# Weight loads of a group issued two periods apart, and the next C chain's x row loaded ahead of the store in SyncE's order

One core of one Trainium2 chip. The metric is the device time of one execution in microseconds (us), the span on the core plus a constant of 1.8 us or so.

## The reference, cut to what matters

```python
def reference(A_x, ..., B_wqkv, B_wo, gate_w):
    x = A_x                                     # 2048 x 1024, bf16
    g = sigmoid((x * gate_w).sum(-1, keepdims=True))
    a = state_space(x, ...)                     # complex scan over 2048 steps, C projection, + x * Dskip
    b = attention(x, B_wqkv, B_wo)              # 32 heads of 32
    return g * a + (1 - g) * b
```

The kernel runs the two branches in one program. Attention is done in 8 groups of 4 heads, with 64 periods to a group; in a period TensorE makes scores, ScalarE (at times with VectorE) exponentiates them, and TensorE fills what is left with the projections and with the state-space branch. The C projection is 32 chains of 16 matmuls. Each chain ends in one 128 x 512 tile in PSUM bank 7.

## The kernel before

A static scheduler in Python emits every instruction with its dependences. Each engine's instructions run in the order of emission, and the waits are put in front of each from the dependences. `p`, the period, is a place in that order.

```python
    def emit(self, eng_name, eng, sems, ...):              # one engine's stream
        for k, o in enumerate(self.q[eng_name]):
            for (l, t) in o.waits:
                eng.wait_ge(sems[l], t * (16 if l.startswith("dma") else 1))
            ins = o.fn(eng)
    # ... cut ...
    def ld_w(self, g, part, eng="sp"):                     # 256 KB of Q, K or V weights, rows of 256 bytes
        ...
        self.S.op(eng, lambda e: e.dma_start(self.w[:, g % 2, part], self.wsrc[:, :, cb:cb + 128]), ...)

    def ld_xn(self, ch, tq, cb):                           # an x row of 128 x 512 in two halves
        for k in range(2):
            self.dma(lambda e, k=k, c0=c0: e.dma_start(self.xn[k], self.x2[...]), [], [("xn", k)] + over, "ld_xn")
        self.c_next += 1

    def skip_ops(self, ch, tq, cb):                        # Ag = x * Dskip * g, two halves, on VectorE
        for k in range(2):
            ops.append((0.335, lambda k=k, c0=c0: self.dve(... self.Ag[:, 0, 256 * k:256 * (k + 1)], self.xn[k] ...
                        [("xn", k), "drow", "g0"], [("Ag", 0)] if k == 0 else [("Ag", 0, 1)], "skip")))
        return ops

    def d_c(self, ch, tq, cb, k):                          # one C chain
        ...
        def evac():
            self.dve(... a = ps[:, 7, :] * g + a ...)      # evac_c: frees bank 7
            self.dma(lambda e: e.dma_start(self.agd[tile], a), [at, ("Ag", 0, 1)], [("agd", tile)], "st_a")
            if self.c_next < 32:
                self.ld_xn(*self.c_list[self.c_next])
    # ... cut: in build(), period p = 64 * g + pg ...
            if pg == (58 if g else 24) and g + 2 < GROUPS:
                for part in (1, 2, 0):
                    self.ld_w(g + 2, part)
```

An evacuation is the VectorE product `evac_c`, which reads bank 7 out; until it has run, TensorE cannot fill the bank again. All of these transfers are issued by SyncE, one after the other; and there is one `Ag` tile, which the skip products write and the stores read.

Of the kernel before, what the change touches and what calls it, by code (L numbers as in the profile page):

```python
# [922 lines left out]
GROUPS = 8  # L923
# [48 lines left out]
class FastPath:  # L972
# [359 lines left out]
    def skip_ops(self, ch, tq, cb):  # L1332

        tt = 4 * ch + tq
        ops = []
        for k in range(2):
            c0 = 512 * cb + 256 * k
            ops.append((0.335, lambda k=k, c0=c0: self.dve(lambda e: e.scalar_tensor_tensor(self.Ag[:, 0, 256 * k:256 * (k + 1)], self.xn[k], self.gcol[:, 0, tt:tt + 1],
                                                                                            self.drow[:, c0:c0 + 256], ALU.mult, ALU.mult),
                                                           [("xn", k), "drow", "g0"], [("Ag", 0)] if k == 0 else [("Ag", 0, 1)], "skip")))  # L1340
        return ops

    def fold_ops(self, j):
# [160 lines left out]
    def d_c(self, ch, tq, cb, k):  # L1504
        ps, xT, cT = self.ps, self.xT, self.cT
        b = self.hp_of[ch]
        hp = self.hp_in[b]
        tt = 4 * ch + tq
        mms = []
        for j in range(8):  # L1510
            for ri in range(2):
                mms.append((1, lambda e, f, l, j=j, ri=ri: e.matmul(ps[:, 7, :], hp(tq, ri, j), cT[ri][:, j, 512 * cb:512 * (cb + 1)], start=f, stop=l),  # L1512
                            [("hp", b, j, ri, tq if b else 0), ("cTf", ri, j)]))


        a = self.Ag[:, 0, :]
        at = ("Ag", 0)
        tile = 2 * tt + cb

        def evac():  # L1520
            self.dve(lambda e: e.scalar_tensor_tensor(a, ps[:, 7, :], self.gcol[:, 0, tt:tt + 1], a, ALU.mult, ALU.add), [("bank", 7), "g0", ("Ag", 0, 1)], [at], "evac_c")  # L1521
            self.dma(lambda e: e.dma_start(self.agd[tile], a), [at, ("Ag", 0, 1)], [("agd", tile)], "st_a")
            if self.c_next < 32:
                self.ld_xn(*self.c_list[self.c_next])
            self.c_left[ch] -= 1
            self.c_end = self.p
        return self.chain(mms, "c", evac)
# [266 lines left out]
    def build(self):  # L1794
# [19 lines left out]
        for j in range(8):  # L1814
            self.bg2 += self.table_ops(j)
        proj = {g: [self.d_qk(g, 1, c) for c in range(4)] + [self.d_v(g, f) for f in range(4)] + [self.d_qk(g, 0, c) for c in range(4)]
                for g in range(1, GROUPS)}
# [27 lines left out]
        outs, k = [], 0  # L1845
# [4 lines left out]
        cur = None  # L1850
# [9 lines left out]
        for p in range(first, NBURST):  # L1860
            g, pg = divmod(p, 64)
# [36 lines left out]
                self.ld_d()  # L1898
                self.ld_xn(*self.c_list[0])

            if pg == (58 if g else 24) and g + 2 < GROUPS:
                assert g or not (proj[0] or cur and cur.tag == "proj")
                for part in (1, 2, 0):
                    self.ld_w(g + 2, part)
            wsv = self.d["B_wo"].rearrange("(a p) n -> p a n", p=128)
            if p == 437:
                self.dma(lambda e: e.dma_start(self.wo3[0], wsv[:, 0:3, :]), [], ["wo0"] + [("w", 0, q) for q in range(3)] + self.x_toks(0), "ld_wo")
# [18 lines left out]
            while used < quota:  # L1926
                if cur is None:
# [16 lines left out]
                    elif kind == "c":  # L1944
                        ok = self.items_done >= 8 * (cs[0][0] + 1) and p > self.item_p + 1 and len(self.folded) == 8

                        def take():
                            self.bgx, self.bgx_at = cs[0][1].pre(), p + 2
                            return cs.pop(0)[1]
# [6 lines left out]
                    cur = take()  # L1956
# [5 lines left out]
                if not cur.pieces:  # L1962
                    ended = cur
                    cur = None
# [247 lines left out]
```

## Time and profile before

| | before |
|---|---|
| time | 924.16 us (median of 3: 923.58 to 925.99) |
| span of the profiled run | 922.4 us |
| busy: ScalarE, TensorE, VectorE | 98%, 98%, 82% |
| ScalarE's waits after the opening and before the end | 3.3 us in five places, 1.0 and 1.6 of them at 246 and 581 us |
| VectorE idle for x rows at the skip products | 12.3 us in 12 places |

In the rows of waits that follow, "A <- B: t, n, m" says that A stood idle t us in all, n times, at most m us, and that B released it. A row of the timeline has start, duration, engine, line, operation, tiles, and in brackets the idle time before it and its releaser. Line numbers above 1340 differ by one to three between the kernels because lines were added and taken out. The granted clock is the share of TensorE's full clock that the trace records as given.

### The profile page before, as it was taken

How to read it: one execution, taken by the hardware profiler on the slowest of the kernel's cores; microseconds unless marked ns; L12 is line 12 of the kernel's file. 1: busy time of each engine (PE TensorE's matmuls, PEld its weight loads, DVE VectorE, ACT ScalarE, POOL GpSimd, SP SyncE). 2: the span in 40 equal slices, each digit the busy share in tenths (PEclk: the TensorE clock that was granted, in tenths of full speed). 3: DMA queues.
4: the chain of work that ended last, by engine and by line, in shares of the span. 5: the costliest groups of instructions: out<-in, count | busy, mean ns of one | idle time of the engine just before them, and what ended most of it. 6: DMA issues, size and time to landing. Idle time of an engine off the chain costs nothing.

```text
span 922.4 us, 33601 instructions
## 1 busy us (share of the span) xinstructions
PE 903.8 (98%) x15188; PEld 515.8 (56%) x15188; DVE 758.1 (82%) x1369; ACT 904.5 (98%) x1034; POOL 6.5 (1%) x31
## 2 busy tenths in 40 slices
PE   8999999999999999999999999999999999999996
PEld 4556655755475555565557555456655655555553
DVE  2799999999989889999889975669989866676665
ACT  6999999999999999999999999999999999999997
POOL 0000000000000000000000000000000000000000
PEclk9999999999999999999999999999999999999999
DMA  9546822223302334122132113123330122533322
GB/s 205 106 83 106 134 50 31 46 45 72 80 9 56 59 62 93 41 41 53 50 82 43 42 40 93 36 69 53 50 65 8 52 76 69 166 87 123 118 65 75
DMA packets 166436, 65.35 MB, mean 71 GB/s; under 512 B 146704, under 2 KB 154896, under 8 KB 166288
## 3 DMA queue, kind: packets, MB, share of 16 engines
q1 hardware_dynamic: 164128, 62.62, 30.8%
q8 instruction: 120, 1.97, 0.9%
q10 hardware_dynamic: 2160, 0.53, 0.3%
q14 instruction: 28, 0.23, 0.1%
HBM read 21.24 MB, written 12.58 MB: 37 GB/s over the span
## 4 chain that ended last, share of the span: by engine, by line
PE 71%; ACT 22%; DVE 4%; SPq 1%; DMA 1%; issue 1%; DVEq 0%
PE f_ps L1766 20%; ACT f_pt L1694 18%; PE f_ps L1678 14%; PE f_ps L1484 12%; PE f_ps L1452 11%; PE f_ps L1512 8%; PE f_ps L1472 6%; ACT f_ub L1717 1%; SPq L1080 1%; DMA f_xa<-in_A_x_dram 1%; DMA f_xT<-in_A_x_dram 1%; ACT f_Et L1694 1%; ACT f_cT_re L1694 1%; DVE f_Ag L1521 1%; ACT f_cT_im L1694 0%
## 5 line engine op out<-in xcount | busy, mean ns | idle before, releaser
L1694 ACT ACTIVATE f_pt<-f_ps 128x1024 bf16<-128x1024 f32 x848 | 801.4, 1138 | 2.7 <-PE f_ps L1678 2.6
L1766 PEld LDWEIGHTS f_ps<-f_V,f_pt 128*128 128x128 bf16 x6784 | 235.0, 96 | 136.6 <-issue 86.6
L1766 PE MATMUL f_ps<-f_V,f_pt 128*128 128x33 bf16 x6784 | 288.4, 178 | 0.2
L1678 PE MATMUL f_ps<-f_Q,f_K 32*128 32x256 bf16 x4096 | 217.7, 273 | 3.9 <-ACT f_cT_re L1694 1.2
L1678 PEld LDWEIGHTS f_ps<-f_Q,f_K 32*128 32x128 bf16 x4096 | 70.2, 92 | 122.8 <-ACT f_pt L1694 62.0
L1484 PE MATMUL f_ps<-f_xT,f_wb 128*128 128x512 bf16 x512 | 131.0, 377 | 1.6 <-DVE f_Ag L1521 0.9
L1452 PE MATMUL f_ps<-f_xT,f_wb 128*128 128x512 bf16 x464 | 119.0, 378 | 3.1 <-DVE f_Ag L1521 3.0
L1398 DVE TENSOR_TENSOR_SCAN f_ht<-f_pf,f_init,f_ut 128x512 bf16<-128x512 f32 x64 | 80.9, 1274 | 0.0
L1512 PE MATMUL f_ps<-f_cT_re,f_hp 128*128 128x512 bf16 x192 | 72.6, 378 | 0.3 <-DVE f_Ag L1521 0.3
L1512 PE MATMUL f_ps<-f_cT_im,f_hp 128*128 128x512 bf16 x192 | 72.5, 378 | 0.0
L1718 DVE TENSOR_SCALAR f_wb<-f_ps 128x512 f32<-128x512 f32 x77 | 52.8, 686 | 23.6 <-PE f_ps L1678 23.0
L1541 PE MATMUL f_ps<-f_wb,f_OT 128*128 128x512 bf16 x252 | 65.5, 378 | 0.0
L1472 PE MATMUL f_ps<-f_wb,f_xT 128*128 128x128 bf16 x896 | 59.1, 219 | 0.0
L1484 PEld LDWEIGHTS f_ps<-f_xT,f_wb 128*128 128x128 bf16 x512 | 40.2, 96 | 33.4 <-issue 1.2
L1717 ACT ACTIVATE f_wb<-f_ps 128x512 bf16<-128x512 f32 x77 | 53.4, 693 | 1.1 <-PE f_ps L1678 1.0
L1452 PEld LDWEIGHTS f_ps<-f_xT,f_wb 128*128 128x128 bf16 x464 | 36.2, 96 | 31.5 <-issue 3.1
L1725 DVE SCALAR_TENSOR_TENSOR f_wb<-f_Ag,f_wb 128x512 int16<-128x512 f32 x77 | 52.6, 684 | 0.7
L1724 DVE SCALAR_TENSOR_TENSOR f_Ag<-f_wb,f_Ag 128x512 f32<-128x512 uint16 x77 | 52.7, 684 | 0.6
L1723 DVE SCALAR_TENSOR_TENSOR f_Ag<-f_wb 128x512 f32<-128x512 uint16 x77 | 52.6, 683 | 0.1
L1472 PEld LDWEIGHTS f_ps<-f_wb,f_xT 128*128 128x128 bf16 x896 | 50.4, 97 | 0.1
L1547 DVE SCALAR_TENSOR_TENSOR f_xT<-f_ps,f_gcol,f_hp 128x512 bf16<-128x512 f32 (+1 forms) x28 | 21.0, 750 | 26.6 <-PE f_ps L1541 26.6
L1390 DVE TENSOR_TENSOR f_tq<-f_ht,f_Et 128x1024 bf16<-128x1024 bf16 x64 | 42.5, 684 | 0.3
(143 smaller groups left out, 876.8 us busy)
## 6 DMA issues: line engine op xcount, KB each, us to landing
ag_scratch<-f_Ag SPq DMA_DIRECT2D x32, 256.0 KB, 2.0
f_hp<-ag_scratch SPq DMA_DIRECT2D x32, 256.0 KB, 2.8
f_wb<-in_B_wqkv_dram SPq DMA_DIRECT2D x21, 256.0 KB, 4.1
out_dram<-f_xT SPq DMA_DIRECT2D x16, 256.0 KB, 2.1
f_xa<-in_A_x_dram SPq DMA_DIRECT2D x32, 64.0 KB, 2.4
f_pf<-in_A_x_dram SPq DMA_DIRECT2D x32, 64.0 KB, 3.2
f_wb<-in_B_wo_dram SPq DMA_DIRECT2D x1, 1024.0 KB
f_OT<-f_On SPq DMA_TRANSPOSE x63, 2.3
```

Of the source, the lines that this page charges most:

```text
L1398: ops.append((1.192, lambda ri=ri: dve(lambda e: e.tensor_tensor_scan(ht[:, ri, :], rr, ut[:, ri, :], self.init[:, ri, j:j + 1], ALU.mult, ...
L1452: mms.append((1, lambda e, f, l, a=a: e.matmul(ps[:, bank, :], w[:, g % 2, part, a, :], xT[:, a, 512 * ch:512 * (ch + 1)], start=f, stop=l ...
L1472: m = e.matmul(ps[:, bank, 128 * q:128 * (q + 1)], xT[:, a, 128 * kt:128 * (kt + 1)], w[:, g % 2, 2, a, :], start=(a == 0), stop=(a == 7))
L1484: mms.append((1, lambda e, f, l, a=a: e.matmul(ps[:, 7, :], bT[:, n % 2, ri, a, :], xT[:, a, 512 * ch:512 * (ch + 1)], start=f, stop=l), [ ...
L1512: mms.append((1, lambda e, f, l, j=j, ri=ri: e.matmul(ps[:, 7, :], hp(tq, ri, j), cT[ri][:, j, 512 * cb:512 * (cb + 1)], start=f, stop=l), ...
L1541: mms.append((1, lambda e, f, l, j=j: e.matmul(ps[:, 7, :], OT[:, j, 256 * qb + 128 * r:256 * qb + 128 * (r + 1)], wo[j][0][:, 512 * cb:51 ...
L1678: m = e.matmul(ps[:, 2 * sl[z] + h % 2, 256 * kl:256 * (kl + 1)], K[32 * h:32 * h + 32, g % 2, 128 * kt:128 * (kt + 1)], Q[32 * h:32 * h + ...
L1694: self.act(lambda e: e.activation(self.tile[p], ps[:, 2 * s:2 * s + 2, :], ACT.Exp, bias=OCTAVES * LN2, scale=LN2 / 128), [("S", s)], [("p ...
L1717: self.S.op("act", lambda e: e.activation(t[:, 0, :], ps[:, 2 * s, :], ACT.Exp, bias=OCTAVES * LN2, scale=LN2 / 128), reads=[("S", s)], wr ...
L1718: self.S.op("dve", lambda e: e.tensor_scalar(xi, ps[:, 2 * s + 1, :], BITS_0, BITS_MIN, ALU.add, ALU.max), reads=[("S", s)], writes=[("xi" ...
L1724: (0.603, lambda: self.dve(lambda e: e.scalar_tensor_tensor(xw, lo, CUBE_C, xw, ALU.add, ALU.mult), [I, W], [W], "exp_c")),
L1766: m = e.matmul(ps[:, 6, o:o + 33], self.tile[p][:, h2, 256 * kl + 128 * qt:256 * kl + 128 * (qt + 1)], V[:, g % 2, 2 * i + kl, h, :], star ...
```

## The change

The intent is that the x row is not late any more: the weights are not to stand in one block in front of it, and it goes out as soon as the buffer that it fills is free.

```diff
@@ skip_ops
+        ops.append((0.0, lambda: self.c_next < 32 and self.ld_xn(*self.c_list[self.c_next])))
         return ops
@@ d_c, evac
             self.dma(lambda e: e.dma_start(self.agd[tile], a), [at, ("Ag", 0, 1)], [("agd", tile)], "st_a")
-            if self.c_next < 32:
-                self.ld_xn(*self.c_list[self.c_next])
             self.c_left[ch] -= 1
@@ build
-            if pg == (58 if g else 24) and g + 2 < GROUPS:
-                assert g or not (proj[0] or cur and cur.tag == "proj")
-                for part in (1, 2, 0):
-                    self.ld_w(g + 2, part)
+            if g + 2 < GROUPS:
+                assert g or pg != 24 or not (proj[0] or cur and cur.tag == "proj")
+                for k, part in enumerate((1, 2, 0)):
+                    if pg == (58 + 2 * k if g else 24):
+                        self.ld_w(g + 2, part)
```

## The prediction

> **What bounds the kernel now.** I read the page first: section 1 and the two large groups of section 5.
>
> ```profile
> PE 903.8 (98%) x15188; PEld 515.8 (56%) x15188; DVE 758.1 (82%) x1369; ACT 904.5 (98%) x1034; POOL 6.5 (1%) x31
> ...
> L1694 ACT ACTIVATE f_pt<-f_ps 128x1024 bf16<-128x1024 f32 x848 | 801.4, 1138 | 2.7 <-PE f_ps L1678 2.6
> ```
>
> ScalarE's exponentials are the pace. One lasts 1138 ns in the record, but in the timeline 15 in a row span 13.99 us, so one starts every 0.91 to 0.93 us and they overlap. I took the starts of all ScalarE instructions from the trace and added up what exceeds 0.933 us after a full exponential and 0.493 us after a half one: most stretches of 30 us lose 0.2 to 0.4 us, but 240 to 270 loses 1.61 and 570 to 600 loses 2.22. So ScalarE bounds the kernel nearly everywhere, and an ScalarE wait in mid-kernel goes straight into the end time. The waits of ScalarE over the whole span are few:
>
> ```profile
> ACT f_pt L1694 <- PE f_ps L1678: 2.6, 4, 1.6
> ACT f_wb L1717 <- PE f_ps L1678: 1.0, 1, 1.0
> ```
>
> The five other rows of that view are the opening (4.5 and 2.7), the last evacuations (1.4 and 0.2) and one of 0.2 near 45 us, which no edited line touches. Asking for the waits in windows of 15 us places the rest: 1.0 at 246, 1.6 at 581, 0.2 at 295, 0.3 at 351, and 0.6 near 10 in the opening. TensorE waits just before each, all for the evacuation of a C chain (L1521): 1.3, 1.6, 0.4 and 0.5 us. Next question: why was that evacuation late? VectorE and the SyncE queue around the largest one:
>
> ```profile
> 569.71 2.06 SPq L1088 DMA_DIRECT2D f_wb<-in_B_wqkv_dram  x3
> 571.81 2.34 SPq L1522 DMA_DIRECT2D ag_scratch<-f_Ag  x1
> 574.19 0.43 SPq L1329 DMA_DIRECT2D f_xa<-in_A_x_dram  x1
> 574.67 0.45 SPq L1329 DMA_DIRECT2D f_pf<-in_A_x_dram  x1
> ...
> 577.08 0.48 DVE L1338 SCALAR_TENSOR_TENSOR f_Ag<-f_xa,f_gcol,f_drow 128x256 f32<-128x256 bf16 x1 [1.81 <-DMA f_xa<-in_A_x_dram]
> 577.49 0.68 DVE L1723 SCALAR_TENSOR_TENSOR f_Ag<-f_wb 128x512 f32<-128x512 uint16 x1
> 578.09 0.47 DVE L1338 SCALAR_TENSOR_TENSOR f_Ag<-f_pf,f_gcol,f_drow 128x256 f32<-128x256 bf16 x1
> 578.49 0.68 DVE L1724 SCALAR_TENSOR_TENSOR f_Ag<-f_wb,f_Ag 128x512 f32<-128x512 uint16 x1
> 579.09 0.74 DVE L1521 SCALAR_TENSOR_TENSOR f_Ag<-f_ps,f_gcol,f_Ag 128x512 f32<-128x512 f32 x1
> ```
>
> The reader sees one queue: three weight loads, the store of the finished C tile, then the two halves of the x row. The store's issue takes 2.34 us where the usual one takes 0.33, so the x row goes out at 574.19; the skip product that needs it idles VectorE for 1.81 us, and the C evacuation stands behind it on the same engine. The chain's last matmul started at 576.82, the evacuation at 579.09: 2.27 us later, where an undisturbed one follows after 0.41. The same happens once more at 234 to 244 (weight loads 234.42 to 236.24, store issue 1.05 us, x row at 237.38, landing after about 3.5 us, skip idle 1.06, evacuation 1.83 us after its last matmul). Of the 32 C chains only these two have a wait for an x row that shows on TensorE. The waits at 295 and 351 have an evacuation 1.1 us late with no wait for a transfer: there the skip products and an exponential's polynomial are simply in front of it.
>
> **What the Trainium skill says.** "Perfetto Trace Analysis", DMA Instruction — HWDGE: the recorded window of such an issue is descriptor generation and its lock, and engines start consuming early when more descriptors are generated than fit the buffer. I read the 2.34 us store issue as that buffer being full of weight descriptors; the trace agrees in that the two stores right behind weights took 1.05 and 2.34 us to issue against a median of 0.33; it does not show the buffer itself. "DMA: Bandwidth & Descriptors", Why small descriptors are slow, charges a fixed cost for each packet; the weight load moves rows of 256 bytes, and its 256 KB land in 4.1 us (median) against 2.0 for a 256 KB C tile with long rows. The same page, Queues, rings and completion order: descriptors of a ring are consumed in order, so an x row behind 768 KB of weights is late; 3.5 and 2.9 us at the two places against a median of 2.4. "PSUM — Partial Sum Buffer", Engine vs sequencer instructions: VectorE's queue is strict FIFO, and the 1.81 us above do hold back an evacuation that does not need the x row.
>
> **The change part by part.** No instruction is added or removed on TensorE, ScalarE or VectorE, and their order is the same: the new entry in the skip list has cost 0 and only issues loads. 62 of the 64 x half-row loads move (the first pair does not), and 10 of the 18 weight loads inside the loop: the second and third of five groups. The group at 51.8 us keeps one period.
> 1. Weight loads at periods 58, 60 and 62 of a group. A period is about 1.85 us (two exponentials), so the second and third go 3.7 and 7.4 us later. Ahead of the store stands one load: 0.58 us of issue in place of 1.8 to 2.06, and a third of the descriptors. The weights are not needed before the next group's first K chain, which starts at about 244.4, against 238.5 for a K part issued at 234.42 with 4.1 us of landing; this part does not move. The Q part, now at about 242, is first read near 279. No new wait there.
> 2. The x row goes out after the second skip product rather than behind the next store. At the first place that product ends near 234.98, so the halves go at about 235.0 and 235.5 (before 237.38, 237.86) and land, with 2.4 to 3.3 us, by 238.8 at the latest; the skip would have started at 240.89 - 1.06 = 239.83. At the second it ends at 570.45, the halves go at 570.5 and 571.0, landing by 574.3; wanted at 577.08 - 1.81 = 575.27. A reserve of 1 us at both.
>
> What that gives. First place: the skip, two products and a sum all move up by 1.06, evacuation at 243.49 - 1.06 = 242.43, that is 0.77 after the last matmul. Chain 1 had 0.69 and cost TensorE nothing, chain 19 had 1.00 and cost 0.31 on TensorE and 0.06 on ScalarE. So 1.01 of ScalarE's wait is won, nearly all. Second place: evacuation at or just after 577.28, 0.46 after the last matmul; all of the 1.58 is won. Sum 2.6 us. Counted by the excess of ScalarE's starts instead, (1.61 - 0.28) + (2.22 - 0.28) = 3.3, but the second stretch contains the small waits that stay. I take 2.7 us. The ten other skip waits for x rows (12.3 - 1.06 - 1.81 = 9.4 us of VectorE's idle time) should mostly go too and be worth nothing, as none reaches TensorE now.
>
> **The rivals.**
> A. The wait returns elsewhere. The x row now waits in SyncE's order for the skip products, so a late skip holds up the store, the attention transposes and the weights behind it; and each later weight load can meet another store. For it: SyncE is one order. Against: stored tiles and transposed outputs are read only in the last 140 us, and the new weight slots at about 242 and 577 have the next x row wanted at 291 and 592. It would leave 0 to 1 us of the gain: 923.2 to 924.2.
> B. The transfers are hidden anyway, the stall only moves: VectorE is 95% busy at 180 to 240 and gets the evacuation late for its own backlog. For it: 0.2 and 0.3 us at 295 and 351 are just that. Against: at 581 it idled 1.81 us directly before. This would save the second place only: 922.6.
> C. More than the two waits: VectorE freed earlier also pulls in the polynomial of the exponentials and thins out the small losses. For it: the 3.3 us count. It makes 920.5 to 921.
>
> **Range and chances.** 924.16 - 2.7 = 921.5. The three runs of before spread over 2.4 us, so a median can be off by about 0.7; with rival B above and C below I take 920.3 to 923.4. Two per cent is 18.5 us, while all of ScalarE's waits outside opening and end are 1.0 + 1.6 + 0.2 + 0.3 + 0.2 = 3.3 us, so faster by 2% is out of reach; slower by 2% would need a new stall repeated many times, or a deadlock.
>
> **What would show it.** Right: no skip product idle for an x row at about 240 and 575; ScalarE's wait rows fall from 2.6 and 1.0 to some 1.0 and 0 (those at 10, 295 and 351 stay); the store issue beside the first weight load back near 0.35 us; x row issued before the store at every C chain. Wrong: a new wait of TensorE on L1521 or L1452 after period 60 or 62 of a group, ScalarE's sum of waits unchanged, or waits of 1 us gone and the span still at 922.

## The result, and the profile after

Six runs each, of the same rounds: after 922.33 us median (921.51 to 922.62), before 925.06 (923.58 to 926.05). The ratio is 0.9970, 95% interval 0.9957 to 0.9983. A ratio here is the mean time of one kernel's runs over that of the other's of the same rounds, so not quite the ratio of the medians. By the medians the change is worth 2.7 us, well inside 2%.

ScalarE's waits over the whole span, the kernel after (the opening's 4.5 and 2.8 us left out, as they are as before):

```profile
ACT f_OT L2069 <- PE f_ps L2066: 1.4, 1, 1.4
ACT f_pt L1693 <- PE f_ps L1677: 1.0, 3, 0.6
ACT f_cT_re L1693 <- PE f_ps L1677: 0.2, 1, 0.2
ACT f_xT L2087 <- PE f_ps L2078: 0.2, 1, 0.2
```

The row of the half exponentials (1.0 us at 246) is gone, and that of the full ones has fallen from 2.6 to 1.0: the waits at 10, 294 and 350 us are left. All idle stretches of ScalarE over 0.05 us but the first one of 4.5 added up are 8.30 us in the kernel before and 5.76 in the kernel after, 2.54 less. (TensorE's busy time reads 884.9 us for 903.8, but 219 matmul records are missing from this trace, 14969 for 15188, so that row is not compared.)

SyncE's queue and VectorE at the place that the prediction showed, one microsecond earlier now; the kernel after:

```profile
568.69 0.57 SPq L1088 DMA_DIRECT2D f_wb<-in_B_wqkv_dram  x1
569.31 0.58 SPq L1329 DMA_DIRECT2D f_xa<-in_A_x_dram  x1
569.93 0.43 SPq L1329 DMA_DIRECT2D f_pf<-in_A_x_dram  x1
570.41 0.43 SPq L1523 DMA_DIRECT2D ag_scratch<-f_Ag  x1
570.88 2.05 SPq L1088 DMA_DIRECT2D f_wb<-in_B_wqkv_dram  x2
...
574.54 0.48 DVE L1338 SCALAR_TENSOR_TENSOR f_Ag<-f_xa,f_gcol,f_drow 128x256 f32<-128x256 bf16 x1 [0.27 <-DMA ag_scratch<-f_Ag]
...
576.54 0.75 DVE L1522 SCALAR_TENSOR_TENSOR f_Ag<-f_ps,f_gcol,f_Ag 128x512 f32<-128x512 f32 x1
```

Three things are to be read here. The x row is out 4.9 us earlier (569.31 for 574.19; 1.0 us of that is the gain of the first place, so 3.9), and the store's issue is back from 2.34 to 0.43 us. The second and third weight load do not come two and four periods later: both are issued at 570.88, right behind the first store, since nothing in front of them in SyncE's order waits for anything. (At the first place they are at 236.55 and 237.03. In the other three groups the second goes 3.4 to 4.8 us after the first and the third right behind it.) And the skip product still waits, 0.27 us, but for another thing: the store of the tile before, which now stands behind the x row. The evacuation starts 0.72 us after its chain's last matmul began, in place of 2.27.

VectorE's waits at the skip products, the kernel before and, in the last line, the kernel after:

```profile
DVE f_Ag L1338 <- DMA f_xa<-in_A_x_dram: 7.9, 9, 2.0
DVE f_Ag L1338 <- DMA f_pf<-in_A_x_dram: 4.3, 3, 1.7
```

```profile
DVE f_Ag L1338 <- DMA ag_scratch<-f_Ag: 1.8, 3, 1.2
```

No skip product waits for an x row any more. 12.3 us have become 1.8, for the store. None of that reaches ScalarE, which had only felt two of the twelve waits.

### The profile page after: what moved, and what is told of

Read it like the earlier page. It is cut to its first block, busy times and chain, and to the rows that moved or that the text cites. A ratio compares the mean times of both kernels' runs of the same rounds, so it can differ in the third digit from the quotient of the medians. Undisturbed runs are those within 1.5% of the kernel's fastest.

```text
span 920.3 us, 33392 instructions
## 1 busy us (share of the span) xinstructions
PE 884.9 (96%) x14969; PEld 516.3 (56%) x15188; DVE 758.0 (82%) x1369; ACT 904.4 (98%) x1034; POOL 6.5 (1%) x31
## 4 chain that ended last, share of the span: by engine, by line
ACT 69%; PE 25%; DVE 2%; SPq 1%; issue 1%; DMA 1%; DVEq 0%
ACT f_pt L1693 59%; PE f_ps L1765 7%; PE f_ps L1677 5%; PE f_ps L1513 4%; PE f_ps L1485 4%; PE f_ps L1453 3%; ACT f_wb L1716 2%; ACT f_OT L1693 2%; ACT f_Et L1693 2%; ACT f_cT_re L1693 2%; ACT f_cT_im L1693 2%; PE f_ps L1473 1%; ACT f_ub L1716 1%; SPq L1080 1%; DMA f_xT<-in_A_x_dram 1%
## 5 line engine op out<-in xcount | busy, mean ns | idle before, releaser
L1765 PEld LDWEIGHTS f_ps<-f_V,f_pt 128*128 128x128 bf16 x6784 | 235.0, 96 | 136.5 <-issue 86.6
L1485 PE MATMUL f_ps<-f_xT,f_wb 128*128 128x512 bf16 x449 | 117.5, 377 | 7.2 <-issue 2.4
L1453 PE MATMUL f_ps<-f_xT,f_wb 128*128 128x512 bf16 x406 | 106.6, 378 | 5.0 <-issue 1.0
L1513 PE MATMUL f_ps<-f_cT_im,f_hp 128*128 128x512 bf16 x183 | 69.1, 378 | 3.0 <-DVE f_Ag L1522 0.5
L1540 PE MATMUL f_ps<-f_wb,f_OT 128*128 128x512 bf16 x219 | 58.0, 378 | 2.1 <-DVE f_xT L1546 0.2
L1513 PE MATMUL f_ps<-f_cT_re,f_hp 128*128 128x512 bf16 x153 | 57.8, 378 | 0.6
```

What stands on the lines that cost most here:

```text
L1453: mms.append((1, lambda e, f, l, a=a: e.matmul(ps[:, bank, :], w[:, g % 2, part, a, :], xT[:, a, 512 * ch:512 * (ch + 1)], start=f, stop=l ...
L1485: mms.append((1, lambda e, f, l, a=a: e.matmul(ps[:, 7, :], bT[:, n % 2, ri, a, :], xT[:, a, 512 * ch:512 * (ch + 1)], start=f, stop=l), [ ...
L1513: mms.append((1, lambda e, f, l, j=j, ri=ri: e.matmul(ps[:, 7, :], hp(tq, ri, j), cT[ri][:, j, 512 * cb:512 * (cb + 1)], start=f, stop=l), ...
L1540: mms.append((1, lambda e, f, l, j=j: e.matmul(ps[:, 7, :], OT[:, j, 256 * qb + 128 * r:256 * qb + 128 * (r + 1)], wo[j][0][:, 512 * cb:51 ...
L1765: m = e.matmul(ps[:, 6, o:o + 33], self.tile[p][:, h2, 256 * kl + 128 * qt:256 * kl + 128 * (qt + 1)], V[:, g % 2, 2 * i + kl, h, :], star ...
```

## The experiments

Twelve runs on the chip, in three jobs. The first job ran on another chip than the second and third, and the kernel before differs from job to job: its median was 926.11 us in the first job (11 runs, 924.43 to 927.67), 924.12 in the second (9 runs, 923.38 to 926.18) and 924.77 in the third (11 runs, 923.38 to 926.81). So times are compared inside a job only. All twelve runs gave the right result. Three kernels could not be run (by my notes; the record keeps nothing of these builds): weights issued from GpSimd on the semaphores that SyncE's transfers use were refused by the simulator, a second `Ag` tile did not fit into SBUF (2048 bytes needed, 576 left), and skip products a period earlier broke an assertion of the scheduler. So what a second `Ag` tile would do to the wait for the store stays untried.

First comes which of the two parts does it; "first place" is the chain that ends near 242, "second place" the one near 577.

### Only the weight periods (spread_only)

The kernel before, with the diff's last part alone.

> Kernel before with the new weight periods alone; the x row stays behind the store. My theory (SyncE order and the weight descriptors ahead of the x row): SyncE's order becomes weight, store, x row, weight, weight, so the store goes out within 0.5 us of the evacuation's end and the x row 0.4 us later, near 236.3 and 571.8; it lands within 2.0 to 2.6 us, before it is wanted (239.8 and 575.3). ScalarE's waits of 1.0 at 246 and 1.6 at 581 vanish; 2.6 us faster than before, the same as the whole change within 0.5. The second and third loads issue directly behind the x row, not two and four periods later, because nothing in front of them waits. Rival (the x row's earlier place is what won): ScalarE's waits of 1.0 and 1.6 stay, time as before.

Measured: 921.92 us against 926.11, ratio 0.9954 (0.9941 to 0.9967). SyncE's queue and the skip product at the second place:

```profile
569.43 0.57 SPq L1088 DMA_DIRECT2D f_wb<-in_B_wqkv_dram  x1
571.07 0.33 SPq L1522 DMA_DIRECT2D ag_scratch<-f_Ag  x1
571.44 0.43 SPq L1329 DMA_DIRECT2D f_xa<-in_A_x_dram  x1
571.91 1.56 SPq L1329 DMA_DIRECT2D f_pf<-in_A_x_dram  x1
573.52 1.06 SPq L1088 DMA_DIRECT2D f_wb<-in_B_wqkv_dram  x2
...
574.92 0.47 DVE L1338 SCALAR_TENSOR_TENSOR f_Ag<-f_xa,f_gcol,f_drow 128x256 f32<-128x256 bf16 x1
```

Both ScalarE waits are gone with the x row still behind the store, and no skip product waits at either place. The x row landed later than I said, though: its last packet ended at 574.79, 3.35 us after the issue and just in time. The rival, that the x row's place won the time, is out. One new small wait of ScalarE is there, 0.3 us at 524, behind a skip product that waits 0.6 us for an x row; the kernel after has none there. So the change's other part is worth that much of ScalarE's waits, too little to show in the times. (Another of 0.3 us, at 17.6, comes before any edited line acts.) The gain in time, 4.2 us, is more than the 2.6 expected; that is taken up below.

### Only the x row's place (xahead_only)

The kernel before, with the diff's first two parts alone.

> Kernel before with the x row ahead of the store alone; three weight loads stay together in front. My theory: the order is three weights, x row, store, so the x row inherits the long issue that the store had (1.05 and 2.34 us), starts near 236.3 and 571.8 and lands near 240.2 and 576.3. First place almost cured (ScalarE wait 0 to 0.4 in place of 1.0), second only in part (0.6 to 1.4 in place of 1.6); 0.8 to 1.8 us faster than before. Rival (the x row's place is what won): both waits gone, 2.6 us faster.

Measured: 926.33 us against 926.11, ratio 1.0003 (0.9988 to 1.0018). Neither theory's number holds: there is no gain at all. The second place:

```profile
570.34 1.91 SPq L1088 DMA_DIRECT2D f_wb<-in_B_wqkv_dram  x3
572.29 2.21 SPq L1329 DMA_DIRECT2D f_xa<-in_A_x_dram  x1
574.55 0.43 SPq L1329 DMA_DIRECT2D f_pf<-in_A_x_dram  x1
575.03 0.43 SPq L1523 DMA_DIRECT2D ag_scratch<-f_Ag  x1
...
577.73 0.48 DVE L1338 SCALAR_TENSOR_TENSOR f_Ag<-f_xa,f_gcol,f_drow 128x256 f32<-128x256 bf16 x1 [1.82 <-DMA ag_scratch<-f_Ag]
```

The x row does inherit the long issue (2.21 us), as expected. What I had left out is the skip product's second need. It overwrites the tile that the store reads, the store now comes after the x row, and it is the store whose landing ends the wait: 1.82 us, where the kernel before waited 1.81 for the x row. The packets in the trace say the same. I counted those of 512 bytes as the x row and those of 2 KB as the store: before, the last x packet ended at 576.92 and the last store packet at 576.53; here they end at 576.65 and 577.29. Weights, x row and store leave SyncE's queue nearly in the order of issue; swapping the last two did not help while three weight loads were in front of both. ScalarE's waits are 1.3 and 2.6 us, more than before; TensorE idled 1.80 and 2.04 us, and after the second its clock was halved (below).

### All three weight loads at period 60 (all_at_60)

```diff
-            if pg == (58 if g else 24) and g + 2 < GROUPS:
+            if pg == (60 if g else 24) and g + 2 < GROUPS:
```

> Kernel before with one number changed: all three weight loads at period 60, none spread, x row behind the store as before. My theory (what counts is what stands in front of the x row in SyncE's order): store and x row go out at once after the evacuation, all three weights right behind them; both ScalarE waits vanish, 2.6 us faster than before, the same as the whole change within 0.5. Rival (spreading itself counts, because three loads in a row saturate the transfers that are in flight beside the x row): the x row lands 3 us or more after its issue and one of the waits stays at over 0.5 us.

Measured: 921.73 us against 926.11, ratio 0.9948 (0.9935 to 0.9961). The second place:

```profile
570.65 0.34 SPq L1522 DMA_DIRECT2D ag_scratch<-f_Ag  x1
571.03 1.51 SPq L1329 DMA_DIRECT2D f_xa<-in_A_x_dram  x1
572.58 0.43 SPq L1329 DMA_DIRECT2D f_pf<-in_A_x_dram  x1
573.06 2.10 SPq L1088 DMA_DIRECT2D f_wb<-in_B_wqkv_dram  x3
```

One number does what the spreading does: in the same job it is within 0.2 us of spread_only, and both ScalarE waits are gone. Half of the rival came true, as the x row's last packet ended 3.25 us after its issue (574.28), but no wait came of it. So it is not the distance between the loads. What counts is how many stand in front of the store and the x row. As in spread_only, a wait of 0.4 us shows at 524.

### Six loads in front (double_w)

The kernel before, and behind each weight load of the five groups another of the same shape, from the same source into a scratch tensor in HBM that nobody reads:

```diff
                     self.ld_w(g + 2, part)
+                    if g:
+                        self.dma(lambda e, g=g, part=part: e.dma_start(self.junk[g, part], self.wsrc[...]), [], [("junk", g, part)], "junk")
```

> Kernel before, with every weight load of the five groups at period 58 followed by another of the same shape into a scratch tensor that nobody reads: six in a row ahead of the store. My theory: the landings of three loads in a row stood 1.0 to 1.2 us apart, so the x row lands about 3.3 us later; ScalarE waits about 4.3 us near 246 and 4.9 us near 581, no other new wait over 0.5 us, 6.6 us slower than before. Rival (the waits at 246 and 581 come of VectorE's own backlog): the waits stay near 1.0 and 1.6, time as before within 1 us.

Measured: 936.8 us against 926.11, ratio 1.0115 (1.0098 to 1.0132). The two rows of ScalarE's waits that hold both places:

```profile
ACT f_pt L1695 <- PE f_ps L1679: 7.8, 5, 6.0
ACT f_wb L1718 <- PE f_ps L1679: 7.5, 2, 6.7
```

The rival (VectorE's own backlog) is out: the waits grow with the loads. My size was too small. ScalarE waited 6.7 and 6.0 us, and 0.8 more after each. TensorE's idle at the two places rose from 1.31 and 1.64 us to 6.10 and 5.42, 4.8 and 3.8 us more, where I had 3.3. At the first place the x row was issued 4.9 us later (242.27 for 237.38), that is 1.6 us for each added load and not the 1.1 that I took from the landings. These loads write HBM, not SBUF, so the dose is not quite of the same kind. The rest I put down to TensorE's clock, which was halved for 6.83 us from within each stall on (from 247.11 and 588.45).

### The kernel before, profiled again (before_again, before_b, before_c, before_d)

Why was the gain 4.2 us in the first job and 2.7 in the first measurement? The kernel before was measured four more times, unchanged.

> The kernel before, unchanged, profiled a second time. The last job measured it at 924.4 to 927.7 while its first profile was of a run of 924.3, and in a variant whose TensorE idled 2.04 us the granted TensorE clock then stood at 0.50 for some 2 us. My theory: the two stalls of the kernel before vary from run to run, and where TensorE's idle exceeds about 2 us its clock halves and the stall costs about 1 us more; so this profile shows ScalarE waits at 246 and 581 of 2.6 us in sum, or 3.5 to 5 us with a window of halved clock behind one of them, and its time is longer by the same amount. Rival (the spread has another origin): the sum of the waits is 2.6 us again within 0.3 whatever the time.

> As before_again, a third profile of the kernel before: ScalarE waits at 246 and 581 between 2.6 and 5 us in sum, the time longer by what exceeds 2.6; a granted clock of 0.5 after every TensorE idle of over 2 us and after none under 1.7 us.

> The kernel before unchanged, a fourth profile. In the last job it ran at 923.4 to 924.3 (one run 926.2) with ScalarE waits of 2.3 to 2.4 us at 246 and 581 and a full clock there; in the job before, on another chip, at 924.4 to 927.7. Theory of the halved clock: a run over 925.5 shows a TensorE idle of about 2 us or more at one of the two places and a granted clock near 0.5 for 2 to 3 us behind it, and a wait of ScalarE larger by about 1 us; a run under 924.5 shows neither. Rival (the slow runs come from elsewhere): the waits at 246 and 581 are 2.3 to 2.7 us in sum in a run over 925.5 too.

> A fifth profile of the kernel before; the same as for before_c.

Measured, one run each: 923.44, 924.02, 926.18 and 923.07 us. ScalarE's waits at the two places were 0.9 and 1.4 us in before_again, 0.8 and 1.5 in before_b, 0.7 and 1.3 in before_d, all with a full clock there: sums of 2.0 to 2.4 us, none of the 3.5 to 5 and at or under the lower edge of the rival's 2.6 within 0.3. In none of them did TensorE idle 2 us (1.56 at most), so they do not decide. The fourth, before_c, is a run over 925.5, as I was looking for. The stretches right behind the two stalls, before_c and then before_d (columns: window and its length; busy time and count of TensorE, its weight loads, VectorE, ScalarE, GpSimd; granted clock; share of the DMA engines; GB/s):

```profile
244.45:247.86 3.41, 3.41 (x23) 1.10 (x22) 2.20 (x3) 1.08 (x3) 0.00 (x0) 0.50 0.34 115
582.37:585.78 3.41, 3.41 (x45) 1.58 (x38) 1.00 (x2) 2.25 (x3) 0.00 (x0) 0.50 0.26 77
```

```profile
244.45:247.86 3.41, 3.35 (x46) 1.57 (x44) 3.08 (x7) 2.69 (x5) 0.00 (x0) 1.00 0.34 115
582.37:585.78 3.41, 3.38 (x59) 1.73 (x56) 3.02 (x8) 3.41 (x6) 0.00 (x0) 1.00 0.11 21
```

With the clock at 0.50, half as many matmuls start in the first stretch (23 for 46), and ScalarE starves: its waits near the two places are 2.33 + 0.20 and 1.58 + 0.78 + 0.07 us, 4.96 in all, against 2.05 in before_d. That is 2.9 us more, and the span is 3.1 us longer (924.4 for 921.3). So the theory of the halved clock fits this run, and its threshold of 2 us falls: TensorE's idle was 1.46 and 1.54 us there, against 1.31 and 1.64 us in the first profile of before, where the clock stayed whole.

Each halved stretch ahead of the last matmuls, in all traces, is 3.41 us long or twice that; the two in before_c begin 337.92 us apart, which is 99 times 3.413 us, and so do the two of the run "four" below. The Trainium skill, "TensorE: Matmul & The Clock Gate", What's actually happening, describes just such a free-running window of 4096 cycles, 3413 ns, that does not start with the kernel, and its half-rate state; the traces agree with the length and with the fixed spacing. It puts the half rate down to an idle window of some 3.4 us; here 1.5 us of idle was enough in one run and not in another. What decides is open. It is not the idle's share of its window: with the windows counted in steps of 3.413 us from the clock changes of each trace, idles of 1.64 us (before, from 578.33) and 1.80 us (xahead_only, from 243.43) each lie inside one window and the clock stayed whole, while those of 1.46 and 1.54 us in before_c lie inside one window too, and it was halved.

So these TensorE stalls of 1.0 to 1.6 us cost ScalarE 0.7 to 1.6 us with a whole clock, and, by my estimate from these pairs, 1.0 to 1.4 us more in before_c, where the clock was halved behind them (2.53 and 2.43 us for stalls of 1.46 and 1.54). The kernel after has no such stall, and its 11 runs (the first measurement and the second job) lie between 921.07 and 922.62, while the kernel before spreads over 923.07 to 927.67. None of the first job's longer runs was profiled, but the record has every run's mean granted clock. Over the three jobs the 14 runs of before above 925.5 us have 0.9960 in the mean (0.994 to 0.998), the 15 at or under 924.6 have 0.9982 (0.996 to 0.999); the halved end of each run is in both. The difference, 0.0022 of 924 us, is what some 4 us at half rate would make. So the longer runs did spend more time at half rate; that it was behind these two stalls is shown in before_c alone.

### The changed kernel again, and with all weights at period 60 (after_again, after_60)

after_again is the kernel after, unchanged. after_60 is that kernel with the edit of all_at_60 in place of the spreading, so that x row, store and three weights follow each other.

> The changed kernel, on one chip with after_60. My theory: no stall, so little spread; 3 to 4.5 us faster than the kernel before on this chip, where before was slower than in the first job, and ScalarE's waits as in the first profile of after (5.8 us in all, opening and end included). Rival (the gain is just the 2.6 us of the first profiles): 2.6 us faster within 0.5.

> The changed kernel with all three weight loads at period 60, so that SyncE's order at the group's end is x row, store, three weights. My theory: nothing of the weights stands in front of x row or store, so the skip product near 575 does not wait for the store either (0.27 us in the changed kernel); ScalarE's waits as in the changed kernel, time the same within 0.5 us. Rival (spreading has a worth of its own): a wait of over 0.3 us on ScalarE at or after 246 or 581, and slower than the changed kernel by over 0.5 us.

Measured: after_again 921.46 us against 924.12, ratio 0.9969 (0.9955 to 0.9982); ScalarE's waits are those of the first profile of after. The gain is 2.7 us here, so the rival's number is met; before had a single run over 925.5 us in this job. after_60: 922.28 us, ratio 0.9977 (0.9963 to 0.9990). As expected, the skip product at the second place no longer waits for the store. But it is 0.8 us slower than after_again, not the same within 0.5. Its waits are as in after_again except the last evacuation, 2.4 us for 1.4, and there the clock was halved (after_60, window and columns as above):

```profile
905.00:908.63 3.63, 2.81 (x60) 1.59 (x58) 3.60 (x6) 3.63 (x5) 0.00 (x0) 1.00 0.39 144
908.63:912.04 3.41, 3.41 (x47) 1.77 (x42) 2.14 (x8) 2.55 (x3) 0.00 (x0) 0.50 0.17 63
```

TensorE had been idle there for no longer than 0.50 us at a stretch, as in after_again, where the clock stayed whole; the weights are 325 us earlier. So I take the wait for the clock's and not for the weights', but the rival, that spreading has a worth of its own, is not out: both of its signs, the longer wait and the 0.8 us, are there, and five runs cannot tell whether this order halves the clock more often. all_at_60 and spread_only were never run beside the kernel after, so which of these is fastest is not shown.

### Two loads in front, and four (two_at_58, four)

two_at_58 is the kernel before with two loads at period 58 and the third at 60. four is the kernel before with one more load, of the unread kind, behind the three.

> Kernel before with two weight loads at period 58 and the third at 60; x row behind the store. Dose below three: one load less in front takes 1.2 to 1.6 us from the x row's landing. The skip near 240 no longer waits, the one near 575 waits 0 to 0.5 us; ScalarE's waits 0 and 0 to 0.4; 2 to 2.6 us faster than a before run without a halved clock. Rival (spreading to one load is needed): ScalarE waits of over 0.5 us stay at either place.

> Kernel before with one further load of the same shape into an unread scratch tensor behind the three weights of each of the five groups: dose of four, x row behind the store. The x row lands 1.2 to 1.6 us later than before; TensorE idles about 3 us at both places[...], so ScalarE waits 2.2 to 3.5 us near 246 and 2.8 to 4.2 us near 581; 3 to 5 us slower than a before run without a halved clock. Without the halved clock the sum would be 2.4 to 3.2 us slower.

Measured, against 924.77: two_at_58 922.22 us, ratio 0.9972 (0.9959 to 0.9984); four 929.4 us, ratio 1.0052 (1.0030 to 1.0075), its runs spread over 927.43 to 931.96.

With two, the first place is cured and the second is not: VectorE still waits 1.1 us for the x row, ScalarE 0.87 (I had said 0 to 0.4, so the rival that one load is the most holds there). By the packets, 240 of the x row's 256 were in at 573.80, the last 16 at 575.17: one sixteenth of the transfer, 1.4 us late. The store's packets show the same, 120 of 128 by 573.30 and eight until 574.78. So the last share, not the mean, sets the landing, and a reserve that I count from the mean landing is too good.

The long issue and the late last share keep company in the traces with something that I overlooked. The page of the kernel before lists a queue whose packets are 16384 bytes each:

```profile
q8 instruction: 120, 1.97, 0.9%
```

One of them moved from 571.68 to 572.88 in two_at_58, and one from 572.50 to 573.64 in the kernel before, in the middle of the store's issue of 2.34 us. At the first place none did (the next began at 240.41); there the store's issue took 1.05 us and the last share was 0.1 us late. Over all 14 traces, from 100 us on, 79 of the 90 SyncE transfers (other than transposes) whose issue took over 1.2 us overlap such a packet, and 265 of the 2212 shorter ones. So the second place's long issue is not the weights' alone. How much each gives was not separated, as no run moved these packets; that the weights decide whether ScalarE waits is shown by spread_only and all_at_60, where such a packet also met an x row's issue (1.56 and 1.51 us) and no wait was left.

With four, ScalarE waits 3.9 and 3.4 us, TensorE idles 2.93 and 2.44 us, and the clock is halved behind both; the time is 4.6 us longer, inside the 3 to 5 of the expectation, though the first wait is above its 3.5.

The dose in one table, ScalarE's waits at the two places in us (x row behind the store in all; a halved clock lies behind the stalls of doses 4 and 6 and, of dose 3, behind those of before_c, 2.3 and 1.6), with the time less that of the kernel before in its job (926.11 for the doses 0, 1 and 6, 924.77 for 2 and 4, so the time column is not one scale):

| loads in front | kernel | first place | second place | time |
|---|---|---|---|---|
| 0 | all_at_60 | 0 | 0 | -4.4 |
| 1 | spread_only | 0 | 0 | -4.2 |
| 2 | two_at_58 | 0 | 0.9 | -2.6 |
| 3 | before, five profiles | 0.7 to 2.3 | 1.3 to 1.6 | 0 |
| 4 | four | 3.9 | 3.4 | +4.6 |
| 6 | double_w | 6.7 | 6.0 | +10.7 |

## Why the prediction was right, point by point

**The time.** 921.5 was predicted and 922.33 measured; the difference to before, 2.7 us, is the one predicted. The kernel before was itself 0.9 us slower in the six runs than in the three that the prediction had. That the gain agrees to a tenth is in part luck: the span fell by 2.1 us in the first profiles, spread_only gained 4.2 us in the first job, and the kernel before varies with a halved clock that the prediction did not know of.

**ScalarE's waits decide.** Right: 2.54 us of its idle time went, and the span fell by 2.1 us in the first profiles (922.4 to 920.3). The waits at 10, 294 and 350 us stayed, as said (by the kernel before's time 10, 295 and 351).

**Part 1, the weights.** The effect was right and the way to it wrong. The step "so the second and third go 3.7 and 7.4 us later" failed: at either place they went 2.2 and 2.7 us after the first, right behind the store. I had taken a place in the order of emission for a time. SyncE issues as soon as nothing in front of it waits. The gain does not depend on it, because the only thing needed was that they no longer stand in front of the store and the x row; all_at_60 shows it. "One load in place of three" was right as the cause: spread_only alone takes both waits away. The reading of the 2.34 us issue as a buffer full of weight descriptors is not shown: in the kernel before, issues of 1.4 to 2.0 us came without weights in front too (1.98 at 516.73), each beside a packet of the instruction queue, and a third store right behind weights, at 350.68, took 0.93 us.

**Part 2, the x row ahead.** The issue times were right (234.97 and 235.59 measured for 235.0 and 235.5; 569.31 and 569.93 for 570.5 and 571.0, less the microsecond won by then). "A reserve of 1 us at both" failed at the second place: the skip product waited 0.27 us in the first profile, for the store. I had counted one of its two needs. For the same reason this part alone is worth nothing (xahead_only), and in the whole change it is worth the 0.3 to 0.4 us wait of ScalarE at 524 that spread_only and all_at_60 show and the kernel after does not.

**The evacuations.** 242.43 predicted, 242.47 measured. At the second place 577.28, less the 1.01 won at the first, is 576.27, and 576.54 was measured: the 0.27 us by which the skip product waited for the store.

**The rivals.** A, a wait that returns elsewhere, exists as the wait for the store, 1.8 us on VectorE and none on ScalarE. B did not come. C, more than the two waits, did not come as I gave it: 922.33 is above its 920.5 to 921. What the two waits do not hold is TensorE's halved clock behind a stall, which no row of waits in the first profile showed because that run had none.

**The other ten waits.** They went and were worth nothing, as said.

## What to carry to other kernels

On an engine that issues transfers in order, a place in the program is not a time: an issue moves up to the last wait in front of it, so ask what stands in front of the urgent transfer, not when the others were meant to go. Before moving a load ahead, list everything that its consumer needs: here the load and the end of a store that reads the consumer's tile, and whichever comes last in the queue sets the time. A stall of TensorE of 1.5 us cost ScalarE 2.5 in a run in which the clock was halved behind it; profile one of a kernel's longest runs as well as one of its shortest before sizing it.

## What the Trainium skill lacked or had wrong

- "TensorE: Matmul & The Clock Gate": it lets the clock fall to half after an idle window of about 3.4 us and advises against gaps above that. Here it fell behind idles of 1.46 and 1.54 us (before_c), stayed whole behind 1.64 us (the first profile of before) and 1.80 us (xahead_only), and fell near the end of after_60 where no idle was over 0.50 us. A later section of the page has short idles between groups of matmuls make the clock swing, but gives no length for them. The window's length, 3.41 us, and that it runs free agree.
- "Perfetto Trace Analysis" says that an issue's recorded window holds descriptor generation; it has no size for what stretches it. The runs: 0.33 us for most stores, 1.05, 0.93 and 2.34 behind three weight loads, 2.21 for an x row's half in the same place. An issue of 1.98 us also came with no weights in front (516.73, the kernel before).
- No page has what a packet of the instruction queue does to SyncE's transfers: 79 of the 90 issues over 1.2 us overlap one. That the one causes the other is not shown.
- "DMA: Bandwidth & Descriptors" has two engines that are usually slower and guesses at GpSimd's queue alone as the cause. Here, on SyncE's, one sixteenth of a transfer lagged too: eight of a store's 128 packets ended 1.8 us after the other 120 (519.34 and 517.54 in the kernel before, with no weights near; a packet of the instruction queue had moved from 516.93 to 518.34).
